# A first pair of token blocks taken from four of eight batches and computed beside the routing, with half-height token reads

## The chip, the cores and the metric

The kernel runs on one core of a Trainium2 chip. The metric is the device time of one execution in microseconds. Where a profile is quoted, PE is TensorE (PEld its weight loads), DVE is VectorE, ACT is ScalarE, POOL is GpSimd and SP is SyncE, which here only issues DMAs.

## The reference

Two parts run one after the other, all in float32. The first is a cross attention between 512 tokens and 32 states, per batch (8) and head (8, of width 64). The second is a mixture of 8 experts over the 544 rows (512 token reads and 32 state reads) of each batch, 4352 rows of width 512.

```python
scores = x @ state.T / 8;  a  = softmax(scores, states);  xread = a  @ state    # 512 rows
scores2 = state @ x.T / 8; a2 = softmax(scores2, tokens); sread = a2 @ x        # 32 rows
x = concat(xread, sread), heads side by side                                   # (8, 544, 512)

logits = x @ w_gate;  local_gate = sigmoid(x @ w_local)
for b in range(B):
    prev_e = -1
    for s in range(S):
        fresh_e = argmax(logits[b, s])
        e = fresh_e if s == 0 or local_gate[b, s] < 0.5 else prev_e
        prev_e = e
        out[b, s] = softmax(logits[b, s])[e] * (relu(x[b, s] @ w1[e]) @ w2[e])
```

A row whose gate is closed takes the expert of the row before it, so the choice is a scan along each batch. w1 is 512 x 1024 and w2 1024 x 512 per expert: 2 MB each.

## The kernel before

**Attention** (class `Attention`, from L180). The order of its steps on all engines is written out by hand in the string `STEPS`: each word is a step and a batch, with half of the heads (`u`) or a portion behind it. For a batch: `xt` and `xn` load x transposed and as it is (SP); `sc` computes the scores on PE; `mx`, `tr`, `mo` (DVE), `sb` (POOL), `ex` (ACT), `zh` (POOL), `zs`, `zi` (DVE), `ml` (POOL) and `tb` (DVE) make the softmax over the states; `et`, `tu`, `ec` and `sr` make the state reads. `lg` and `lt` give the logits of the token rows, `sl` and `sk` those of the state rows. `vv` computes the token reads (`token_reads`, L428): for each 128 tokens two matmuls, whose stationary operand is the shares `a` of four heads (4 x 32 = 128 rows) and whose moving operand `sd` holds those heads' states on the diagonal of a 128 x 256 matrix that is zero elsewhere. `xr` (ACT) copies the result, `wr` (SP) writes it to `rows`, a tensor in DRAM. The word `go` leaves the string; `reads()` goes on with it from the routing code, so that token reads of the last batches stand among the routing's instructions.

**Routing** (class `Routing`). When the logits of batches 0 to 6 are there, `choose` picks the largest for each row (L521 to L527), and again for batch 7. From there a serial chain runs, mostly on DVE: transposes, the scan along each batch (L557), one-hots of the expert, counts by matmul, the number of full 256-row pairs for each expert, the number of 32-row tiles for the rest, and a slot for each row (L642 to L661). One-hots of the slots, multiplied on PE (`slotted`, L710), turn slots into lists of rows: first for the first two blocks alone (`slots.two`), then for all blocks (`slots.tok`). `keep` (L538) issues dummy matmuls whose results nobody reads.

**Experts** (`experts`). Rows of one expert are worked off in pairs of blocks, 2 x 128 rows. POOL gathers a pair's rows (L821; `tick`, L835, ties a gather to a result on PE), SP loads the weights in quarters (L873). The first pair is multiplied in the plain way (`plain`, L1097), and its rows are gathered whole (L827) and turned on PE (`turned`, L856). Each later pair uses seven products of halves in place of eight (`strassen`, L1013, and `second_half`, L1053). Nine small tiles of 32 rows run between the first pairs. At least 10 pairs run unconditionally; each further one stands in a `tc.If` on the number of pairs (`last`). An indirect DMA on POOL scatters a block's 128 result rows to the output (L996). In the conditional pairs, the gather for the pair after next is issued before it is known whether that pair will run, and each scatter waits for the one before it to land, since both write `out`.

Of the kernel before, what the change touches and what calls it, by code (L numbers as in the profile page):

```python
# [40 lines left out]
NB = NP * 2  # L41
NBLK = NB + (NTILE + Q - 1) // Q
# [8 lines left out]
def kernel(  # L51
# [41 lines left out]
    route = Routing(ctx, tc)  # L93

    with ExitStack() as phase, ExitStack() as late:
        p = late.enter_context(tc.tile_pool(name="p", bufs=4, space=PSUM, side="right"))
        reads = late.enter_context(tc.tile_pool(name="reads", bufs=1, side="right"))
        lt = reads.tile([P, B, NC, SQ], F32, name="lt")
        with ExitStack() as early:
            make_identity(nc, ident)  # L100
            start = Attention(early, tc, p, reads, xn, xt, st, stt, wgl, wgs, lt, rows, none)
            route.constants(ident)
            start.clear()
            route.more_constants()
            start.run(route)
        bank = Banks(tc, 4)
        routing = route.route(bank, lt, slots, start.reads, rows)
        experts(phase, late, tc, bank, w1, w2, rows, slots, route, routing, out)
# [19 lines left out]
class Slots:  # L128


    def __init__(self, pool):

        self.tok = pool.tile([P, NBLK], I32, name="tok")
        self.two = pool.tile([P, 2], I32, name="two")

# [7 lines left out]
        self.experts = pool.tile([1, NP + NTILE - 1], I32, name="experts")  # L143
# [7 lines left out]
sc0 kp3 xt11 xt10 mx00 ga kp2 sd3 tr01 xt21 mx01 sd2 mo01 nb0 tr00 et01 sb01 xn0 mo00 wm14 sc1 et00 sb00 ex01  # L151
iv0 tu01 tr11 gl tu00 zh01 ex00 tr10 xt20 ec00 zh00 zs01 mo10 sd0 xn1 zs00 sb10 zi0 ec01 mx11 sd1 sr0 ml01 mo11
ex10 mx10 sc2 ml00 st0 xt30 tb01 rt0 sb11 tb00 sl0 xt31 tr20 lg0 nb1 ex11 zh10 sk0 tr21 vv03 et10 zh11 xt41 zs10
vv00 et11 lt0 mx21 xr03 xt51 zs11 tu11 zi1 xr00 tu10 iv1 ml11 mo21 vv02 xt50 ec10 mo20 ml10 sc3 ec11 tb11 xt40
xr02 mx20 sb21 sr1 tb10 xn2 tr30 sb20 ex21 lg1 mx30 st1 vv12 zh21 ex20 rt1 tr31 nb2 sl1 zh20 et20 vv10 zs21 sk1
lt1 ws1 zs20 et21 tu20 zi2 xt60 mo30 xr10 ml20 sc4 xr12 iv2 mx31 ec20 xn3 ml21 tu21 tb20 vv11 mx41 ec21 nb3 sb30
et30 tb21 sr2 tr40 et31 xt61 lg2 mo31 ex30 tu30 mo40 sb31 st2 sc5 lt2 wr00 xr11 mx40 ec30 zh30 tr41 wr03 tu31
ex31 nb4 zs30 sb40 vv23 et40 mx50 xt70 ec31 mo41 tu40 zh31 ex40 rt2 sr3 sb41 zs31 ws0 xr23 zi3 xn5 et41 iv3 sl2
ml31 mx51 vv22 ex41 sk2 iv4 st3 ml30 tb31 sc6 xr22 rt3 ec40 zh41 tb30 xt71 sl3 zh40 zs41 lg3 tr50 nb5 vv31 wr02
zs40 et50 zi4 vv01 xn4 lt3 xr31 ml40 mo50 sk3 tr51 xr01 vv13 ml41 tb40 et51 vv21 mo51 sb50 xr13 wr10 iv5 vv20  # L160
tb41 xr21 sb51 xn6 mx60 ex50 lg4 mx61 xr20 zh50 tu50 ex51 lt4 tu41 tr60 nb6 ec50 zh51 tu51 zs50 et60 mo60 vv32
wr20 ec51 zs51 sb60 zi5 tu60 ec41 wr23 tr61 sc7 xr32 ml50 wr11 ex60 mo61 sr4 et61 ml51 tb50 wr12 mx71 sr5 sb61
ws2 st4 tb51 ec60 ws3 vv30 tr70 zh60 ex61 xn7 mx70 st5 lg5 zh61 xr30 zs60 tu61 mo70 nb7 et70 vv40 zs61 sb70 zi6
ec61 tu70 lt5 wr22 iv6 xr40 ml61 rt5 sr6 rt4 ex70 tr71 wr40 ec70 ml60 mo71 sl5 et71 wr13 sl4 sk5 tb61 vv41 sb71
st6 wr31 tb60 tu71 zh70 ex71 sk4 iv7 wr32 lg6 rt6 xr41 zs70 zh71 sl6 ec71 lt6 wr21 vv42 zs71 zi7 wr01 sr7 sk6
xr42 ml71 ch0 wr42 vv33 st7 ml70 wr41 vv50 tb71 xr33 wr33 tb70 vv53 xr50 rt7 wr30 lg7 xr53 sl7 lt7 wr53 vv51 sk7
go wr50 vv43 xr51 wr51 go xr43 vv52 wr43 vv61 xr52 ws4 vv60 wr52 xr61 go ws5 xr60 vv62 wr60 go xr62 ws7 wr62
vv71 wr61 vv72 xr71 wr71 vv63 xr72 wr72 vv70 xr63 go wr63 go xr70 wr70 ws6 go vv73 xr73 wr73
# [3 lines left out]
class Attention:  # L172


    def __init__(self, ctx, tc, p, late, xn, xt, st, stt, wgl, wgs, lt, rows, none):
# [5 lines left out]
        self.xp = ctx.enter_context(tc.tile_pool(name="xp", bufs=3))  # L181
# [8 lines left out]
        self.sttc = [once.tile([P, n, KT, N], F32, name=f"sttc{i}") for i, n in enumerate((1, B - 1))]  # L190
# [3 lines left out]
        self.states_of = once.tile([P, B * G * DH], F32, name="states_of")  # L194
        nc.sync.dma_start(out=self.states_of, in_=st)
        nc.sync.dma_start(out=self.sttc[1], in_=stt[:, 1:])
        nc.sync.dma_start(out=wgs.rearrange("p w k e -> p (w k e)"), in_=wgl)
# [3 lines left out]
        self.sd = late.tile([P, B, G * GD], F32, name="sd", bufs=1)  # L201
# [10 lines left out]
    def clear(self):  # L212
# [5 lines left out]
        nc.gpsimd.memset(self.gl, 0.0)  # L218
        nc.gpsimd.memset(self.lt, 0.0)
        nc.gpsimd.memset(self.sd, 0.0)  # L220
# [9 lines left out]
    def reads(self):  # L230
# [7 lines left out]
                  sd=self.diagonal, ga=self.gates, gl=self.gates_kept, ch=self.choose, kp=self.keep, wm=self.warmed)  # L238
# [6 lines left out]
    def bank(self, parts=P, n=512):  # L245
        return self.p.tile([parts, n], F32, tag="p", name="p")
# [15 lines left out]
    def choose(self, i):  # L262
        self.route.choose(self.lt, 0, B - 1)

    def diagonal(self, k):
        r = slice(32 * k, 32 * k + 32)
        to = self.sd[r].rearrange("p b (g d) -> p b g d", g=G)
        self.nc.scalar.copy(to[:, :, :, DH * k:DH * k + DH],
                            self.states_of[r].rearrange("p (b g d) -> p b g d", b=B, g=G))

    def load_t(self, b, h):
        x = self.new(self.xp, f"x_t{h}", (b,), [P, KT // 2, S])
        self.nc.sync.dma_start(out=x.rearrange("p k s -> p (k s)"), in_=self.xt[b][:, h * D * 2:(h + 1) * D * 2])

    def load_n(self, b):
        x = self.new(self.xp, "x_n", (b,), [P, SC, G, KT, DH])
        self.nc.sync.dma_start(out=x.rearrange("p c u k d -> p (c u k d)"), in_=self.xn[b])

    def states(self, b):
        return self.sttc[b > 0][:, b - (b > 0)]  # L280
# [102 lines left out]
    def state_reads(self, b):  # L383
# [3 lines left out]
        for u in range(G):  # L387
            for c in range(SC):
                for k in range(KT):
                    self.nc.tensor.matmul(r[32 * k:32 * k + 32, u, :], lhsT=e[:, c, u, 32 * k:32 * k + 32],  # L390
                                          rhs=x_n[:, c, u, k, :], start=(c == 0), stop=(c == SC - 1))
# [36 lines left out]
    def token_reads(self, b, c):  # L428
        v = self.of["v", b, c] = self.bank()
        for u in range(G):  # L430
            d = slice(u * GD, u * GD + GD)
            self.nc.tensor.matmul(v[:, d], lhsT=self.get("a", b, u)[:, c * P:c * P + P], rhs=self.sd[:, b, d],  # L432
                                  start=True, stop=True)

    def reads_kept(self, b, c):
        xr = self.new(self.late, "xr", (b, c), [P, D], bufs=12)
        v = self.get("v", b, c)
        self.nc.scalar.copy(xr.rearrange("p (k u d) -> p u k d", k=KT, u=G),  # L438
                            v.rearrange("p (u k d) -> p u k d", u=G, k=KT))

    def reads_to_rows(self, b, c):
# [3 lines left out]
        t = b * T + c * P  # L445
        self.nc.sync.dma_start(out=self.rows[t:t + P].rearrange("t q x -> t (q x)"), in_=self.get("xr", b, c))
# [783 lines left out]
```

## Time and profile before

| | |
|---|---|
| median of 3 runs | 550.08 us (547.25 to 551.04) |
| the profiled execution | 546.65 us |
| its span, first to last instruction | 544.9 us |
| PE busy | 524.6 us (96%) |
| DVE busy | 382.5 us (70%) |
| POOL busy | 313.0 us (57%) |
| ACT busy | 174.0 us (32%) |
| moved by DMA | 155.48 MB, 285 GB/s over the span |
| mean granted PE clock | 0.987 |

The span is divided by what runs in it: attention to 68 us, routing to 95 us, expert pairs to 535 us, and the last scatters. An engine's share over the whole span says little, since the stages have different limits; the busy times by stretch are what to read. "Busy" for PE counts dummy matmuls too. Matmul ends are modelled, so the price of a matmul is better read from the distance of two starts, or from a long group's time divided by its count, than from a mean duration.

### The profile page before, as it was taken

To read this page: it belongs to the slowest core of one execution; us is meant where nothing else is said; L and a number is where in the kernel's file an instruction comes from. 1 tells how busy PE (TensorE), PEld (TensorE's weight loads), DVE (VectorE), ACT (ScalarE), POOL (GpSimd) and SP (SyncE) were. 2 spreads that over 40 slices of the span, in tenths; PEclk is the share of its full clock that TensorE was granted. 3 is DMA by queue.
4 is the path that set the end of the run, shared out by engine and by line. 5 is a ranking of instruction groups with operands and counts; after the bars stand their busy time and mean duration, and the time that the engine had idled before them with its cause. 6 is when DMAs were issued, how large, how long until landed. Compare 5 with 4: busy or idle time off the path is not lost. (4 is left out here: it accounts for less than half of the span.)

```text
span 544.9 us, 12958 instructions
## 1 busy us (share of the span) xinstructions
PE 524.6 (96%) x4916; PEld 459.3 (84%) x4916; DVE 382.5 (70%) x623; ACT 174.0 (32%) x359; POOL 313.0 (57%) x386
## 2 busy tenths in 40 slices
PE   8799898999999999999999999999999999999992
PEld 2567766989989898989898989899999998999992
DVE  6999876738575667575756658495776777777763
ACT  6788654111313232222222222223222221322230
POOL 7788602655574567565655556446565655445555
PEclk9999998999999999999999999999999999999997
DMA  8999766799989898898989898874748475565742
GB/s 320 410 350 350 294 237 214 275 397 390 377 284 387 299 376 322 327 369 299 375 294 369 293 366 299 320 251 142 259 142 302 134 276 178 216 218 205 248 151 99
DMA packets 49003, 155.48 MB, mean 285 GB/s; under 512 B 6865, under 2 KB 8017, under 8 KB 45602
## 3 DMA queue, kind: packets, MB, share of 16 engines
q1 hardware_dynamic: 41234, 135.78, 68.5%
q0 software_dynamic: 7552, 18.69, 9.6%
q8 instruction: 42, 0.69, 0.5%
q14 instruction: 31, 0.25, 0.1%
q10 hardware_dynamic: 144, 0.07, 0.1%
HBM read 136.68 MB, written 17.89 MB: 284 GB/s over the span
## 5 line engine op out<-in xcount | busy, mean ns | idle before, releaser
L821 POOL DMA_INDIRECT xg<-rows,row x132 | 157.4, 1192 | 29.5 <-issue 27.3
L930 DVE TENSOR_TENSOR a<-a,a 128x1024 f32<-128x1024 f32 x64 | 77.0, 1223 | 31.2 <-DMA a<-in_w_dram 29.8
L1013 PE MATMUL ps<-xt,a 128*128 128x128 f32 x720 | 88.6, 276 | 0.0
L1013 PE MATMUL sum<-xs,a 128*128 128x128 f32 x720 | 87.7, 275 | 0.0
L1013 PEld LDWEIGHTS ps<-xt,a 128*128 128x128 f32 x720 | 84.4, 192 | 2.1 <-issue 1.8
L1013 PEld LDWEIGHTS sum<-xs,a 128*128 128x128 f32 x720 | 84.0, 192 | 0.0
L930 DVE TENSOR_TENSOR c<-c,c 128x1024 f32<-128x1024 f32 x64 | 75.4, 1219 | 3.7 <-DMA c<-in_w_dram 3.2
L1053 PE MATMUL ps<-c,h 128*128 128x256 f32 x312 | 74.7, 382 | 0.0
L1053 PEld LDWEIGHTS ps<-c,h 128*128 128x128 f32 x312 | 58.0, 190 | 10.9 <-issue 3.7
L996 POOL DMA_INDIRECT out_dram<-y,tok x32 | 35.0, 1093 | 52.8 <-issue 16.8
L1053 PE MATMUL ps<-c,hs 128*128 128x256 f32 x256 | 60.5, 379 | 0.0
L1053 PEld LDWEIGHTS ps<-c,hs 128*128 128x128 f32 x256 | 48.6, 190 | 6.6
L1053 PE MATMUL sum<-c,h 128*128 128x256 f32 x200 | 47.2, 379 | 0.0
L930 DVE TENSOR_TENSOR h<-s,s 128x512 f32<-128x512 f32 x15 | 10.4, 693 | 51.5 <-ACT s L1036 48.2
L1053 PEld LDWEIGHTS sum<-c,h 128*128 128x128 f32 x200 | 38.0, 190 | 5.2
L849 DVE STREAM_TRANSPOSE xt<-xg 128x512 f32<-128x512 f32 x32 | 34.2, 1091 | 8.4 <-DMA xg<-rows,row 8.4
L964 ACT COPY sum<-ps 128x256 f32<-128x256 f32 (+1 forms) x31 | 14.3, 460 | 71.1 <-PE ps L1013 49.5
L835 POOL COPY tick<-s 1x1 f32<-1x1 f32 x45 | 15.9, 354 | 36.3 <-ACT s L1036 36.3
L835 POOL COPY tick<-r 1x1 f32<-1x1 f32 x41 | 17.2, 419 | 30.5 <-ACT r L1058 22.9
L432 PE MATMUL p<-sd,a 128*128 128x256 f32 x128 | 32.1, 390 | 0.2 <-ACT xr L438 0.2
L1058 ACT ACTIVATE r<-sum,prob 128x256 f32<-128x256 f32 x32 | 15.1, 473 | 52.0 <-PE sum L1053 49.5
L1053 PE MATMUL sum<-c,hs 128*128 128x256 f32 x128 | 30.2, 379 | 0.0
(230 smaller groups left out, 757.8 us busy)
## 6 DMA issues: line engine op xcount, KB each, us to landing
a<-in_w_dram SPq DMA_DIRECT2D x68, 512.0 KB
c<-in_w_dram SPq DMA_DIRECT2D x68, 512.0 KB
at<-in_w_dram SPq DMA_DIRECT2D x18, 1024.0 KB
ct<-in_w_dram SPq DMA_DIRECT2D x18, 1024.0 KB
x_t<-in_xt_dram SPq DMA_DIRECT2D x16, 512.0 KB
x_n<-in_xn_dram SPq DMA_DIRECT2D x8, 1024.0 KB
rows<-xr SPq DMA_DIRECT2D x32, 256.0 KB
xg<-rows,row POOLq DMA_INDIRECT x132, 5.7
```

The source lines that it names most:

```text
L432: self.nc.tensor.matmul(v[:, d], lhsT=self.get("a", b, u)[:, c * P:c * P + P], rhs=self.sd[:, b, d], start=True, stop=True)
L821: nc.gpsimd.indirect_dma_start(out=to.rearrange("p x k -> p (x k)"), out_offset=None, in_=rows.rearrange("n q x -> (n q) x"), in_offset=ba ...
L835: nc.gpsimd.tensor_copy(tick, value)
L849: nc.vector.transpose(to.rearrange("p k (i t) -> p k i t", i=Q), xgs_[u % 2][:, b].rearrange("p i x k -> p k i x"))
L930: nc.vector.tensor_tensor(out, a, b, op=op)
L964: nc.scalar.copy(y, x)
L996: nc.gpsimd.indirect_dma_start(out=out, out_offset=to, in_=y, in_offset=None, bounds_check=NT - 1, oob_is_err=False)
L1013: nc.tensor.matmul(to[:, m * P:m * P + P], lhsT=w[:, j, m * P:m * P + P], rhs=x[:, j, :], start=begin and m == 0 and j == 0, stop=(m == FK ...
L1053: nc.tensor.matmul(to, lhsT=x[:, m, :], rhs=w[:, m, :], start=begin and m == 0, stop=(m == FK // 2 - 1), skip_group_check=True)
L1058: nc.scalar.activation(to, t, Act.Copy, scale=p)
```

## The change

1. The commonest expert among the token rows of batches 0 to 3 is found as soon as these batches have logits (`EB` = 4). Its first 256 rows are gathered, its weights loaded into the buffers that held x, and both layers are computed in the plain way while attention and routing go on (class `Early`, new). The results wait in `ye`; they are scaled and scattered inside the first pair of the loop, when the probabilities are known.
2. The routing of all rows leaves these 256 rows out and counts one pair as done (the scan over pairs starts at 1.0). The loop has one pair less; its first pair is still computed in the plain way.
3. Token reads work on two heads at a time: 64 rows of `a` against a 64 x 128 block of `sd`, in the upper and lower half of the array, into two PSUM banks. `sd` is loaded by four DMAs into the two diagonal halves, in place of four ACT copies. Rows are written 256 at a time.
4. `STEPS` is a new string, and the early pair's steps stand in it, also behind the `go`s. The `keep(22)` and `keep(3)` of the routing are gone.
5. At the end: scatters in the conditional pairs are declared independent of each other, and a pair's last gather for a pair that may not run moves behind the `tc.If`. The tiles s and r of a pair share buffers.

```diff
-sc0 kp3 xt11 xt10 mx00 ga kp2 sd3 tr01 xt21 mx01 sd2 mo01 nb0 tr00 et01 sb01 xn0 mo00 wm14 sc1 et00 sb00 ex01
+lb lc sc0 kp3 la xt10 mx01 mx00 xt11 tr00 ga nb0 mo00 et00 xt20 tr01 sb00 gl tu00 mo01 et01 xn0 sb01 ex00 sc1
...
+wr31 fc ml41 kp4 tu50 ml40 mo50 ec50 wr21 fd tb41 sc6 fe sb50 ff tb40 xn4 fg ex50 mx60 lg4 fh zh50 vv41 lt4 fi
...
+fo xt71 rt4 sb51 tr60 sl4 sr5 fp et60 xn6 sk4 mo60 fq ex51 tu60 tr61 st5 mo61 et61 rt5 kp1 sc7 ec60 zh51 iv6
...
+ws7 tb71 pp011 wr50 sk7 cc lg7 cd ce pp012 lt7 wc1 go pp013 wc2 go rl01 vv60 wc3 pp100 xr601 xr600 pp101 wc0 go
+vv61 wr60 pp102 xr610 xr611 go pp103 wr61 pp000 rl10 pp001 pp002 vv71 go go qq1000 xr711 xr710 pp003 wr71 go
+qq1001 rl00 vv70 qq0000 xr701 xr700 qq0001 qq1010 wr70 go qq0010 qq0011 go qq0100 qq1011 qq1100 go qq1101 go
+qq1110 qq1111 qq0101 ye1 qq0110 qq0111 ye0
...
-        self.sd = late.tile([P, B, G * GD], F32, name="sd", bufs=1)
+        self.sd = late.tile([P, B, G, 2, DH], F32, name="sd", bufs=1)
...
+    def load_states(self):
+        st = self.inputs[1].rearrange("p (b u d) -> p b u d", b=B, u=G)
+        for k in range(KT):
+            r = slice(32 * k, 32 * k + 32)
+            self.nc.sync.dma_start(out=self.sd[r, :, :, k % 2, :], in_=st[r])
...
+    def token_reads(self, b, j):
+        v = self.of["v", b, j] = [self.bank().rearrange("p (c k u d) -> p c k u d", c=2, k=2, u=G) for h in range(2)]
+        for c in range(2):
+            t = slice((2 * j + c) * P, (2 * j + c) * P + P)
+            for u in range(G):
+                for h in range(2):
+                    r = slice(64 * h, 64 * h + 64)
+                    self.nc.tensor.matmul(v[h][:, c, :, u, :], lhsT=self.get("a", b, u)[r, t], rhs=self.sd[r, b, u],
+                                          start=True, stop=True)
...
+class Early:
...
+    def gather(self):
+        for k in range(2):
+            self.nc.gpsimd.indirect_dma_start(
+                out=self.first[k], out_offset=None, in_=self.rows[:EB * T].rearrange("n q x -> n (q x)"),
+                in_offset=bass.IndirectOffsetOnAxis(ap=self.slots.first[:, k:k + 1], axis=0))
...
+    def one(self, b, n, i):
+        if i == 0:
+            self.hps[b, n] = self.bank()
+        for j in range(KT):
+            self.nc.tensor.matmul(self.hps[b, n][:, i * P:i * P + P], lhsT=self.ring[0][2 * n + j // 2][:, j % 2, i * P:i * P + P],
+                                  rhs=self.x_t[:, j, b * P:b * P + P], start=(j == 0), stop=(j == KT - 1))
...
+    def two(self, b, n, o, s):
+        if (n, o, s) == (0, 0, 0):
+            self.yps[b] = self.bank()
+        for m in range(2 * s, 2 * s + 2):
+            self.nc.tensor.matmul(self.yps[b][:, o * D // 2:o * D // 2 + D // 2], lhsT=self.h[2 * b + n][:, m, :],
+                                  rhs=self.ring[1][2 * n + o][:, m, :], start=(n, o, m) == (0, 0, 0),
+                                  stop=(n == 1 and m == FK // 2 - 1), skip_group_check=True)
...
-        nc.vector.tensor_tensor_scan(end[:, 0], on[:, 0, 1:E + 1], pairs, 0.0, Alu.mult, Alu.add)
+        nc.vector.tensor_tensor_scan(end[:, 0], on[:, 0, 1:E + 1], pairs, 1.0, Alu.mult, Alu.add)
...
-        reads()
-        keep(22)
...
-        keep(3)
...
     next(routing)
+    load(0, 0)
+    gather_first()
+    next(routing)
+    reads()
+    turned_first(0)
+    next(routing)
+    reads()
     late.close()
...
+        if apart:
+            tc.declare_no_dep(put.ins, group="scatters", reason="a token has one slot, so scatters write other rows")
+            tc.add_to_no_dep_group("scatters", put.ins)
...
+                for b in range(2):
+                    nc.scalar.activation(early.ys[b], early.ys[b], Act.Copy, scale=slots.prob[:, b:b + 1])
+                    scatter(b, early.ys[b])
...
+        if not late:
+            calls = iter(range(NP))
+            gets[1] = lambda value: rest(value) if next(calls) < Q - 1 else None
```

In the new string, `fa` to `fr` are the early routing (transposes, scan, one-hots, counts, the commonest expert, ranks, place masks, list of rows, gather), `wa` and `wc` load its weights, `ta` and `tc` turn the gathered rows, each `pp` is four written matmuls of the first layer, each `qq` two of the second, `rl` and `ye` the copies behind them.

## The prediction

> **What bounds the kernel now.** First the page's slices, for where TensorE is short of work:
>
> ```profile
> span 544.9 us, 12958 instructions
> ...
> PE   8799898999999999999999999999999999999992
> ...
> PEclk9999998999999999999999999999999999999997
> DMA  8999766799989898898989898874748475565742
> ```
>
> From slice 8 (about 100 us) to the last one PE is full, so there the time is PE's work. The page's chain of waits holds 5% of the span and all of that in the tail, so it can't tell about the start. For that I took the busy times by stretch (columns: stretch, its length, busy us and count of PE, PEld, DVE, ACT, POOL, granted clock, DMA share, GB/s):
>
> ```profile
> 0.00:8.00 8.00, 6.15 (x26) 1.60 (x27) 4.22 (x18) 3.60 (x12) 6.73 (x13) 1.00 0.72 247
> 8.00:62.20 54.20, 49.27 (x1001) 33.89 (x1001) 51.28 (x123) 44.89 (x101) 43.34 (x54) 1.00 0.98 372
> 62.20:68.30 6.10, 5.11 (x103) 4.23 (x103) 5.09 (x13) 2.86 (x6) 2.26 (x2) 1.00 0.63 233
> 68.30:95.05 26.75, 23.93 (x174) 17.39 (x173) 19.12 (x64) 13.32 (x31) 2.96 (x3) 0.92 0.65 227
> 95.05:111.20 16.15, 16.15 (x136) 16.15 (x135) 11.93 (x22) 2.69 (x6) 10.40 (x11) 0.92 0.81 286
> ```
>
> Attention (8 to 68.3) is bound by DVE (56.4 busy of 60.3) with DMA close behind (0.98 up to 62.2). From 68.3, where the last batch's experts are chosen, to 95.05, where the first expert matmul starts, a serial routing chain runs; PE's 23.9 there are about 14 of token reads and 6.3 of dummy matmuls (L538). After that PE alone counts. Third, PE's timeline, for the unit prices:
>
> ```profile
> 95.08 5.08 PE L1097 MATMUL ps<-xt,a 128*128 128x128 f32 x32
> ...
> 100.47 10.88 PE L1097 MATMUL ps<-xt,a 128*128 128x128 f32 x96
> ```
> ```profile
> 485.80 1.95 PE L1013 MATMUL ps<-xt,a 128*128 128x128 f32 x16
> ...
> 508.66 1.89 PE L1053 MATMUL ps<-c,h 128*128 128x256 f32 x8
> 510.39 1.95 PE L1013 MATMUL ps<-xt,a 128*128 128x128 f32 x16
> ```
>
> A seven-product pair repeats after 510.39 - 485.80 = 24.6 us. A 128-column record takes 10.88/96 = 0.113 (0.159 in the first 32, under the lower clock), a 256-column one (510.39 - 508.66)/8 = 0.216. Each written fp32 matmul is two records. Last, two views for the edits: PE's groups up to 105 us, and the end of POOL.
>
> ```profile
> L432 PE MATMUL p<-sd,a 128*128 128x256 f32 x128 | 32.1, 390 | 0.2 <-ACT xr L438 0.2
> ...
> L307 PE MATMUL s<-x_t,sttc 64*32 64x512 f32 x128 | 9.8, 601 | 0.7 <-DMA x_t<-in_xt_dram 0.7
> ```
> ```profile
> 535.04 1.02 POOL L996 DMA_INDIRECT out_dram<-y,tok  x1 [0.30 <-issue]
> 536.03 0.81 POOL L835 COPY tick<-y 1x1 f32<-1x1 f32 x1
> 537.00 1.80 POOL L821 DMA_INDIRECT xg<-rows,row  x1 [0.16 <-issue]
> 540.07 1.02 POOL L996 DMA_INDIRECT out_dram<-y,tok  x1 [1.27 <-DMA out_dram<-y,tok]
> ```
>
> PE ends at 535.15; the last scatter goes out at 540.07, behind a gather that nobody will use and the landing of the scatter before it.
>
> **A pair less in the full stretch: -24.6.** The before trace holds 720/48 = 15 seven-product pairs and one plain one. Worked through the reference, the commonest expert of the first four batches has 512 token rows, so the early pair is full, its expert's remainder stays what it was, and the loop runs 15 pairs in place of 16. The first pair of the loop stays plain, so one seven-product pair goes.
>
> **Attention gets longer: +5.5 on DVE, +1 at the start.** Added before the last batch's choice, priced by the same operation in the old routing: a scan over 512 columns 1.2 (the 8x544 one took 1.27), one-hots 0.25 (half of 0.49), two place masks 1.25 (four took 2.49), some 14 small operations at 0.15 to 0.2, 2.4; choosing in three portions instead of two 0.4. Sum 5.5, on the bound engine. The lower end is 1.6, if it falls in the 3.9 that DVE idles between 8 and 68.3; I take 5.5, since those idles are waits of 0.2 to 1 us that new operations don't fit. ScalarE loses the four diagonal copies (4.2) and gains about 7 of copies and activations by the end of attention; it has 9 free. POOL gets two gathers at 1.1 and three small operations, about 3, in 11 free. At the start SP now waits for a halved clear of the state tile (3.5/2, ending near 4.0) and issues four loads (about 0.45 each) ahead of batch 1's x, which it issued at 3.47 before and near 6.5 now. Batch 1's scores ran at 12.15 on that load, with DVE idle 1.0 for them. Bounds 0 to +3; I take +1, as less is queued beside it. The logits of batch 7, 67.1 before, then run at 73.6.
>
> DMA has to agree: issued up to batch 7's x are 8.4 MB of transposed x, 6.3 of the other, 4.2 of finished rows and 1.3 of states, 20.2 MB. With 2.8 moved by 10 us and 0.39 MB/us after that (before: 281 GB/s in the first 10 us, 351 to 415 in the next four stretches of 10), that is 55 us. Some 40 DVE operations of 0.45 follow it, so 73 to 74. At 0.36 it is 58, and everything 3 later.
>
> **Token reads.** 128 records of 256 columns (27.7 at 0.216) become 256 of 128 columns on half of the rows. If two halves run side by side, 13.8 to 14.5; if not, 28.9. L307's 64x32 tiles are the nearest row: 16 records of 512 columns took 1.09, where 16 x 0.432 = 6.9 would be serial, so halves and columns do overlap; I take 1.0 for each group of 16, 16 in all. Of these 12 lie in attention, beside DVE, and gain nothing; 4 lie in routing. In L307, 16 weight loads took 0.18, or 11 ns each, so loads of separate tiles overlap too.
> The Trainium skill, "TensorE: Matmul & The Clock Gate", section "LDWEIGHTS (loading the stationary operand)", speaks against this edit: a load costs its columns at 1.2 per ns, however few rows it has. By that 256 loads of 128 columns are about 27 us (an estimate from that page), the edit gains nothing, and the routing stretch is 2.8 longer; L307's 11 ns, where the rule gives 27, is why I don't take it.
>
> **The routing stretch becomes PE-bound: 26.75 to about 38.** PE keeps its order, and behind batch 7's logits it now has: 10 early steps of 8 records (0.91) = 9.1; 16 of 4 records of 256 columns (0.864) = 13.8; four token reads 4.0; the logits 1.0; the chain's own matmuls 9.3 (transposes 0.57 and 0.42, counts 0.6, ends and experts 0.46, 40 for two blocks 2.0, 40 for all blocks 3.9, quarter rows 0.54, turns and bank claims about 0.9). Sum 37.2, plus 1 for hand-overs. The new work is cut into portions of 0.9 to 6 us between chain steps, each about the DVE work there (3.3 of count arithmetic beside 4.6, 6 of slot arithmetic beside 6.2), so DVE hides behind PE. The 25 removed dummies are worth 0: the matmul behind them waited for DVE at 85. First loop matmul at 73.6 + 38.2 = 111.8, against 95.05: **+16.7**. Bounds: 104 (DVE additions hidden, gaps none) and 122 (start +3, DMA +3, reads serial +3, hand-overs +1).
>
> **First plain layer: -1.2.** It took 16.15; at full clock with both blocks there, 128 x 0.113 and 0.6 of turns is 15. The early pair's scaling (two ScalarE copies near 0.6) and two scatters (2.1) go into POOL's 5.7 free there; uncovered they cost 2.
>
> **Tail: -3.9.** Without the unused gather and the wait between scatters, the last one goes out near 536.2 instead of 540.07.
>
> **Sum.** +16.7 - 24.6 - 1.2 - 3.9 = -13.0. The profiled execution was 546.65 (span 544.9 and 1.75 around it), so 533.6 for its like; the median of the runs shown is 3.4 above it, so 537 for the median.
>
> **Rivals.**
> *POOL stalls (slower).* The early gather needs the rows of four batches in DRAM, and behind it on POOL stand the subtractions and shares of batches 5 to 7, for which DVE and ScalarE wait. The rows' last write is about 17 MB into the queue, 46 us; the gather is due near 54. If it waits, each us of it moves everything: from 13 on the change loses. Before, the wait of the token read (L719) for the rows was 18.7, though with nothing behind it. With 20 lost, 557. Against it: 8 us of slack.
> *PSUM instead of PE.* A token read now takes two of four banks, and an early product holds one; if each of 16 reads waits for a 0.58 copy, +9, and 546.
> *Reads don't overlap.* +3 in routing and up to 3 in attention: 541 to 543.
> *Early routing is hidden.* Loop from 104: 529.
>
> **How the numbers follow.** Forecast, 532 to 542 with the serial reads in it: 0.60. Hidden: 0.10. PSUM or late DMA, 544.6 to 551: 0.16. POOL stall or the like, above 555.6 mostly: 0.14. Range 529 to 551 leaves out about 0.2. A measurement here can tell 1%, 5.5 us: faster 0.70, same 0.16, slower 0.14.
>
> **What would show it.** After: 14 seven-product pairs spaced 24.6; batch 7's logits near 74; the first loop matmul near 112 with PE full and clock 1.00 before it; L468 groups of 16 near 1.0 us; two final scatters about 1 us apart. Wrong, if the logits come after 80, if PE idles over 5 us between them and the loop, or if POOL waits for rows before the early gather.

## The result and the profile after

The changed kernel took 551.34 us (median of 20 runs, 549.15 to 556.11), the kernel before 549.48 us (20 runs) beside it: a ratio of 1.0049, 95% interval 1.0026 to 1.0073. Forecast were 537 us and a gain of 2.4%. So a loss of half a per cent came of it, within what the text called no change. The profiled execution took 551.26 us, its span is 549.5, against 546.65 and 544.9 before.

The page of the changed kernel, its span and the slices of PE, its granted clock and the DMA engines (each digit is a fortieth of the span, in tenths):

```profile
span 549.5 us, 13280 instructions
...
PE   6998899999989999999999999999999999999995
...
PEclk9898899999999999999999999999999999999998
DMA  9999899469969798998979797978646483846662
```

PE is full from slice 6 (69 us) on but for slice 12 (151 to 165 us), which is looked at below. So the loss is in what comes ahead of the loop and in how much shorter the loop became. The same kernel by stretches up to the first loop matmul, which starts at 122.59 (95.05 before); the columns are the stretch, its length, the busy time of each engine, PE's granted clock, the DMA share and GB/s:

```profile
0.00:8.00 8.00, 6.17 (x26) 1.61 (x27) 2.88 (x20) 3.60 (x12) 5.01 (x13) 1.00 0.73 215
8.00:74.40 66.40, 57.27 (x1147) 36.97 (x1145) 56.09 (x138) 43.08 (x103) 42.69 (x55) 0.92 0.95 327
74.40:83.95 9.55, 9.28 (x157) 8.51 (x157) 6.21 (x20) 5.14 (x12) 6.30 (x7) 1.00 0.98 343
83.95:97.00 13.05, 13.05 (x145) 12.02 (x146) 8.19 (x34) 4.20 (x10) 0.00 (x0) 1.00 0.87 306
97.00:122.59 25.59, 23.60 (x194) 20.28 (x190) 16.80 (x53) 10.12 (x23) 3.97 (x4) 1.00 0.54 177
sum 122.59, PE 109.38 PEld 79.39 DVE 90.17 ACT 66.14 POOL 57.97; mean PE 21.88 PEld 15.88 DVE 18.03 ACT 13.23 POOL 11.59
```

The early pair's first product starts at 74.3 and batch 7's logits at 83.95 (67.08 before). Read the third row against the others: from 74.4 on PE is busy in 45.9 of 48.2 us, and DVE, which set the pace of attention before, is not. And read the sum: up to the loop PE is busy for 109.4 us, against 84.5 of 95.05 before. Of the 27.5 us by which the loop starts later, 24.9 are PE's busy time and 2.6 its idle time. That is a sum and not yet a cause. Over attention alone, from 8 us to batch 7's logits, neither engine is full; the rows are before, after, and e4, a kernel of the experiments that is the same up to these logits:

```profile
8.00:67.08 59.08, 53.16 (x1077) 37.05 (x1078) 55.99 (x132) 47.75 (x107) 45.60 (x56) 1.00 0.95 360
8.00:83.95 75.95, 66.56 (x1303) 45.48 (x1301) 62.30 (x157) 48.22 (x114) 48.99 (x61) 0.93 0.96 329
8.00:83.66 75.66, 63.44 (x1300) 44.23 (x1298) 62.28 (x157) 48.37 (x114) 48.93 (x61) 1.00 0.96 331
```

What PE does there, groups of matmuls between 8 us and the loop (records, then busy time and mean ns, then idle time before them), first before, then after:

```profile
L432 PE MATMUL p<-sd,a 128*128 128x256 f32 x128 | 32.1, 390 | 0.2 <-ACT xr L438 0.2
...
L307 PE MATMUL s<-x_t,sttc 64*32 64x512 f32 x112 | 7.6, 601 | 0.1
```

```profile
L468 PE MATMUL p<-sd,a 64*128 64x128 f32 x256 | 18.2, 283 | 0.1
L643 PE MATMUL p<-xt,x 128*128 128x128 f32 x128 | 16.4, 280 | 0.3 <-DMA x<-in_w_dram 0.3
L653 PE MATMUL p<-x,h 128*128 128x256 f32 x64 | 15.3, 387 | 1.2 <-ACT h L647 1.2
L339 PE MATMUL s<-x,sttc 64*32 64x512 f32 x114 | 12.9, 780 | 0.6 <-DMA x<-in_xt_dram 0.6
```

The token reads give back 13.9 us (32.1 to 18.2), the early pair's two layers cost 31.7, and the scores, which the change doesn't touch, cost 5.3 more: a batch's 16 records take 1.09 us when both halves of x have landed, but batch 4's came as two runs of eight, 1.5 us apart, and took 2.56, and batch 7's took 1.96 while the granted clock was 0.61 (65 to 69 us).

From there to the end the two kernels compare like this:

| | before | after | difference | forecast |
|---|---|---|---|---|
| first loop matmul | 95.05 | 122.59 | +27.5 | +16.7 |
| of it: batch 7's logits | 67.08 | 83.95 | +16.9 | +6.5 |
| of it: logits to loop | 27.97 | 38.64 | +10.7 | +10.2 |
| first plain layer | 16.14 | 14.84 | -1.3 | -1.2 |
| rest of the loop | 423.96 | 405.29 | -18.7 | -24.6 |
| last matmul to the end | 9.75 | 6.8 | -2.9 | -3.9 |
| span | 544.9 | 549.5 | +4.6 | -13.0 |

The rest of the loop falls short by 5.9, and here is where, in the order of time on PE in the changed kernel (start, duration, group, idle time before it):

```profile
157.04 0.25 PE L1006 MATMUL ps<-pd,turn 128*128 128x9 bf16 x4
157.22 1.29 PE L1159 MATMUL ps<-ct,htt 128*32 128x128 f32 x39
158.79 0.43 PE L1159 MATMUL ps<-ct,htt 128*32 128x128 f32 x5 [0.28 <-issue]
159.52 0.43 PE L1159 MATMUL ps<-ct,htt 128*32 128x128 f32 x4 [0.30 <-issue]
160.26 0.44 PE L1159 MATMUL ps<-ct,htt 128*32 128x128 f32 x6 [0.31 <-issue]
```

The 64 matmuls of a tile's second layer took 1.95 us at each of the nine tiles in the trace of before. Here the first takes 5.65, and four others 2.1 to 3.0; the nine sum to 23.1 us against 17.6. "Issue" says that PE waited for nothing that the profile shows.

The tail on POOL after:

```profile
538.84 0.97 POOL L1094 DMA_INDIRECT xg<-rows,row  x1 [0.38 <-issue]
540.13 1.02 POOL L1239 DMA_INDIRECT out_dram<-y,tok  x1 [0.32 <-DVE y L1319]
543.60 1.73 POOL L1239 DMA_INDIRECT out_dram<-y,tok  x1 [2.44 <-DVE y L1326]
```

The unused gather and the wait for the first scatter's landing are gone. The second scatter now waits for DVE's last result and goes out 3.5 us after the first, not 1.

### The profile page after: what moved, and what is told of

It reads as the page before. It is cut to its first block, busy times and chain, and to the rows that moved or that the text cites. A ratio compares the mean times of both kernels' runs of the same rounds, so it can differ in the third digit from the quotient of the medians.

```text
span 549.5 us, 13280 instructions
## 1 busy us (share of the span) xinstructions
PE 527.2 (96%) x5104; PEld 458.2 (83%) x5104; DVE 369.2 (67%) x633; ACT 169.5 (31%) x357; POOL 311.3 (57%) x373
## 4 chain that ended last, share of the span: by engine, by line
PE 87%; DMA 5%; DVE 4%; issue 1%; SPq 1%; POOL 1%; ACT 0%; POOLq 0%; ACTq 0%; DVEq 0%
PE ps L1299 21%; PE ps L1259 19%; PE sum L1259 14%; PE sum L1299 12%; PE ps L1159 4%; PE ps L1147 3%; PE ps L1343 3%; PE p L643 3%; PE p L653 2%; DMA x<-in_xn_dram 2%; DMA x<-in_xt_dram 2%; PE ps L942 2%; PE s L339 1%; DMA x<-in_w_dram 1%; PE p L468 1%
## 5 line engine op out<-in xcount | busy, mean ns | idle before, releaser
L1259 PE MATMUL sum<-xs,x 128*128 128x128 f32 x608 | 74.1, 275 | 0.0
L1259 PE MATMUL ps<-xt,x 128*128 128x128 f32 x592 | 73.3, 277 | 0.0
L1259 PEld LDWEIGHTS ps<-xt,x 128*128 128x128 f32 x592 | 69.6, 192 | 1.9 <-issue 1.4
L1259 PEld LDWEIGHTS sum<-xs,x 128*128 128x128 f32 x608 | 70.9, 192 | 0.0
L1173 DVE TENSOR_TENSOR x<-x,x 128x1024 f32<-128x1024 f32 x49 | 59.1, 1220 | 10.9 <-DMA x<-in_w_dram 9.9
L1239 POOL DMA_INDIRECT out_dram<-y,tok x30 | 36.6, 1219 | 17.6 <-DVE y L1326 9.6
L1103 POOL COPY tick<-r 1x1 f32<-1x1 f32 x38 | 17.8, 469 | 38.2 <-ACT r L1304 35.6
L1299 PE MATMUL ps<-c,h 128*128 128x256 f32 x160 | 38.3, 382 | 0.0
L1299 PEld LDWEIGHTS ps<-c,h 128*128 128x128 f32 x160 | 29.8, 190 | 5.8 <-issue 2.1
L1299 PE MATMUL ps<-c,hs 128*128 128x256 f32 x144 | 34.0, 379 | 0.0
L1299 PE MATMUL ps<-x,h 128*128 128x256 f32 x136 | 32.6, 382 | 0.0
L1299 PEld LDWEIGHTS ps<-x,h 128*128 128x128 f32 x136 | 25.3, 190 | 4.8 <-issue 1.6
```

The costliest lines, as they stand in the source:

```text
L1103: nc.gpsimd.tensor_copy(tick, value)
L1173: nc.vector.tensor_tensor(out, a, b, op=op)
L1239: put = nc.gpsimd.indirect_dma_start(out=out, out_offset=to, in_=y, in_offset=None, bounds_check=NT - 1, oob_is_err=False)
L1259: nc.tensor.matmul(to[:, m * P:m * P + P], lhsT=w[:, j, m * P:m * P + P], rhs=x[:, j, :], start=begin and m == 0 and j == 0, stop=(m == FK ...
L1299: nc.tensor.matmul(to, lhsT=x[:, m, :], rhs=w[:, m, :], start=begin and m == 0, stop=(m == FK // 2 - 1), skip_group_check=True)
```

## The experiments

All times of milestones are from one profiled execution each. Five of the kernels here are the same up to the loop (the changed kernel, and those altered in the loop only). In the four of them that are used for it, batch 7's logits run from 81.58 to 83.95 and the loop starts from 120.23 to 122.59: differences below 2.4 us in these two say nothing.

**Is it the loads?** Three kernels. e1 loads the states in one DMA of long runs, with four ScalarE copies into the diagonal in their place:

```diff
-        for k in range(KT):
-            self.nc.sync.dma_start(out=self.sd[r, :, :, k % 2, :], in_=st[r])
+        self.nc.sync.dma_start(out=self.states_of, in_=self.inputs[1])
+    def diagonal(self, k):
+        self.nc.scalar.copy(self.sd[r, :, :, k % 2, :],
+                            self.states_of[r].rearrange("p (b u d) -> p b u d", b=B, u=G))
```

> The changed kernel with its states loaded as before, in one DMA of 4 KB runs, and put on the diagonal halves by four ACT copies. Theory A (late x: the end of attention is set by when the x of the late batches lands): the four loads of 64-float runs held the DMA engines at a share of 1.24 for 240 GB/s between 8 and 12 us, where the kernel before moved 416; 0.7 MB less there and 0.3 MB less between 4 and 8 us are worth about 2.5 us, so the logits of batch 7 come at 81 to 82 instead of 83.95, and the total falls by 2 to 3 us. Theory B (attention is set by VectorE's added work and by the order of steps): the logits stay within 1 us of 83.95.

Logits at 82.16, loop at 120.80, 551.14 us against 550.26 (ratio 1.0019, 0.9987 to 1.0051): within the spread. e2 leaves out 2 MB of the loads:

```diff
+            if h == 0 or b not in (3, 4, 5, 6):
                 self.nc.sync.dma_start(out=x, in_=self.xn[b][:, h * D * 2:(h + 1) * D * 2])
```

> The changed kernel without the second half of the x loads for the state reads of batches 3 to 6 (the matmuls run on the values that are in the buffers): 2 MB less, 1.5 MB of it ahead of batch 7's transposed x. Theory A: at the 0.34 MB/us that the changed kernel moved between 10 and 64 us, that x lands 4.4 us earlier and the logits of batch 7 come at 79 to 80. Theory B: 83 to 84, since no VectorE instruction and no step of the order is changed.

Logits at 82.84, loop at 121.48. The DMA share from 60 to 72 us fell from 0.80 to 0.49 and nothing beyond the spread followed from it, so the bytes don't set attention's end. e3 moves steps of batches 6 and 7 up in the order:

```diff
 xt60
+xt61 xt70
...
 wr30
+xt71
...
+sc7
 fo
...
 tr61
+mx70
 mo61
+mx71
```

> The changed kernel with the transposed x of batches 6 and 7 issued before the rows of batches 2 and 3 on SP, and with batch 7's scores and maxima moved up in the order of steps. Theory A with SP's order as the cause: batch 7's scores run near 58 to 60 instead of 65.86, its logits 3 to 6 us earlier (78 to 81), the total falls by as much. Theory A with the sum of bytes as the cause: what is moved ahead pushes the rest back, so the scores come earlier, the logits at 83 to 85. Theory B: as the latter.

Logits at 88.33, loop at 126.95, ratio 1.0136 (1.0037 to 1.0235; four runs). The one load moved up (batch 7's scores came at 64.58) pushed the others back: PE waited 4.4 us for batch 4's natural x. e8 moved the load of the states behind batch 0's natural x:

```diff
-lb lc sc0 kp3 la
+lb sc0 kp3 la
...
 xn0
+lc
```

> The changed kernel with the load of the states (four DMAs of short runs) moved from the first place in SyncE's queue to behind batch 0's natural x, so that it no longer stands ahead of batch 1's transposed x. If that load is what makes batch 1's scores 1.9 us late (14.04 us against 12.16), sc1 comes at 12.0 to 12.6 and batch 3's logits at 43 rather than 44.9. What follows for batch 7: theory A' (loads) gives 82 us for its logits, theory C 83 to 84, since the early chain starts from batch 3's logits but batches 4 to 7 then wait for the chain all the same: the two differ by no more than the spread of the milestones here, so this run only prices the start, at 0 to 2 us.

Batch 1's scores came at 11.27, 2.8 us earlier, and the clock in 12 to 24 us was 1.00 in place of 0.86; the logits stayed at 83.88, the loop at 122.52. The better start is lost again long before batch 7: batch 3's logits came at 45.01, against 43.66 in the changed kernel.

**Is it PE's own work?** e4 leaves 12 of the 16 early second-layer steps out:

```diff
+        if n or s:
+            return
         for m in range(2 * s, 2 * s + 2):
```

> The changed kernel without 12 of the 16 steps of the early pair's second layer (48 records of 256 columns, 10.4 us of PE). If PE bounds the stretch from batch 7's logits to the first loop matmul, 38.6 us falls to 28 or 29. If the serial chain on VectorE or the hand-overs bound it, it stays above 35.

Logits at 83.66, loop at 117.17, 33.5 us behind them in place of 38.6: of 10.4 us taken away 5.1 were gained. PE was then busy in 15.3 of the last 20.2 us, at a granted clock of 0.80 in place of 1.00, so part of the loss may be the clock. With that said, PE's work is not all that holds the stretch: some of it is the routing's chain of steps.

**Is it the early choice, or the token reads?** Four kernels make a table of the two. e7 drops the choice and takes fixed rows and expert 0; e13 drops the reads of batches 0 to 3; e12 drops both; e11 drops the choice and e2's 2 MB.

```diff
-        return dict(fa=self.sequence, fb=self.holds, fc=self.filled, fd=self.back, fe=self.experts_kept,
+        return dict(fa=self.fixed, **{f"f{c}": lambda: None for c in "bcdefghijklmnopr"}, fq=self.gather,
...
```

```diff
+        for name in ("vv", "xr", "wr"):
+            do[name] = lambda b, *at, step=do[name]: step(b, *at) if b >= EB else None
```

> The changed kernel without its early choice: the steps from the sequence to the chosen slots are left out, the first pair takes rows 0 to 255 and expert 0, and the later routing counts all tokens (so the first pair's rows of the output are not the reference's). All loads, all attention steps, the token reads, the gather and the first pair's products stay. Theory C (the early routing chain, 6.3 us of DVE work and its hand-overs from engine to engine, stands in order between the steps of batches 4 to 7 and holds them up): batch 7's logits come at 77 us or earlier (83.95 in the changed kernel), the loop's first matmul at 113 to 117. Theory A' (the later loads and the order of steps alone set the end of attention): logits at 82 to 84, loop at 120 or later. DVE's busy time from 44 to 84 us falls by about 6 us under either.

> Both suspects taken away at once: no early choice (as e7) and the second half of natural x of batches 3 to 6 left out (as e2, 2 MB less). Each alone moved batch 7's logits by 1.1 to 1.4 us only (82.56 and 82.84 against 83.95). Theory G (two chains of about the same length, the DMA queue's and the early routing's, so that either alone holds the end): logits at 77 or earlier. Rival H (neither is the limit; the token reads of batches 0 to 3, which now stand within the attention stage with their ScalarE copies and their writes in SyncE's queue, hold the loads behind them): logits at 80 to 82.

> No early choice (as e7), and the token reads of batches 0 to 3 with their copies left out; their rows are written as zeros after the attention stage, and the early gather takes its rows from natural x. So the attention stage holds nothing of the change but the loads in halves, the order of steps and the first pair's products. Theory H: logits of batch 7 at 68 to 72 (67.08 before). Rival G, or an order of steps that is slow in itself: 76 or later.

> The early choice stays, the token reads of batches 0 to 3 are left out (as e12, with zeros written afterwards and the early gather from natural x). Theory H alone: logits of batch 7 at 74 to 76, that is those of e12 and the 5 to 6 us of the early choice's VectorE work. If the early choice holds batches 4 to 7 up by its waits once the loads are on time: 79 or later.

| batch 7's logits | with the choice | without |
|---|---|---|
| with the reads | 83.95 | 82.56 (and 82.12 without 2 MB of loads) |
| without the reads of batches 0 to 3 | 81.62 | 78.72 |

Theories C, G and H fall, each by its own number: the choice alone is within the spread, and even without choice and reads the logits come 11.6 us later than before. The choice costs 2.9 us once the reads are out, the reads 3.8 once the choice is out, and both together 5.2. (e12's and e13's loop and time are not read: the zeros written behind attention delay the routing.)

**Is it a milestone at all?** e15 moves the six early product steps that stand ahead of batch 7's logits behind them; e14 leaves the fillers out. Both have an edit in the loop as well, read further below.

In `STEPS`, first e15, then e14 (what stands between these words is left as it is):

```diff
-pp110 pp111 pp112 pp113 rl11 pp010 pp011
...
 lg7
+pp110 pp111 pp112 pp113 rl11 pp010 pp011
```

```diff
-kp3 kp5 kp2 kp4 kp2 kp1 kp1
```

> Two edits. The six early product steps that stand ahead of batch 7's logits on PE (6.3 us) are moved behind them. Theory P: the logits come 5 to 6 us earlier, near 78, and the loop starts where it did, 121 to 124, since PE has the same work before it. Rival O (batch 7's logits set the loop, 38.6 us behind them): the loop starts at 115 to 118. In the loop, the last tile's scatter stands apart (as e10): on a chip where the tenth seven-product pair is late (27.8 to 31.4 us in e7 to e9), theory F gives 24.6 here and 27 or more for e14.

> Two edits at places far apart. In the attention stage the filler matmuls (18 of 0.39 us, 5.3 us of PE in the changed kernel's trace, which compute nothing) are left out. Theory P (PE's own work sets the start of the loop): the first loop matmul comes 3 to 5 us earlier, 118 to 120, with batch 7's logits at 80 to 82. Rival O (the order of steps and its waits set it): PE idles instead, the loop stays at 121 to 123; if the fillers hold up the clock, it comes later than 123. In the loop, the early pair's two scatters stand behind the third pair (as e9). On a chip where the tiles' second layer is slow, theory D gives 2.0 to 2.6 us for the first tile's here and about 5 for e15's; rival D' gives 5 for both.

e15's logits of batch 7 came in two halves, the last at 81.38, 2.6 us earlier, and its loop started 2.6 us later, at 125.17. Its row for 72 to 84 us, and e14's for 12 to 24 (columns as above):

```profile
72.00:84.00 12.00, 8.92 (x160) 7.36 (x159) 9.04 (x30) 5.34 (x12) 7.47 (x9) 0.86 1.00 367
```

```profile
8.00:12.00 4.00, 0.24 (x8) 0.15 (x8) 3.71 (x6) 0.78 (x2) 1.43 (x3) 0.88 1.23 239
12.00:24.00 12.00, 10.38 (x232) 5.67 (x232) 7.36 (x16) 6.30 (x16) 7.32 (x9) 0.64 0.95 379
```

In e15 PE idles 3.1 us where the product steps had stood, and has them still to do afterwards: the loop starts 43.8 us behind the logits instead of 38.6. Had the logits alone set the loop, it would have started 2.6 us earlier. e14's 5.3 us of fillers less made the logits (86.42) and the loop (125.06) 2.5 us later, just outside the spread, so theory P, that PE's work alone sets the loop, falls too: without the fillers PE's clock was 0.64 from 12 to 24 us and 0.72 from 48 to 72, against 0.74 to 0.86 and 0.86 to 1.00 in five kernels that have them (the changed one, e9, e10, e15 and e18). The Trainium skill, "TensorE: Matmul & The Clock Gate", section "What's actually happening", says that the array falls to half its clock after an idle window of some 3.4 us; the row of 0.24 us busy in 4 and the one behind it fit that.

The milestone is one where the order is kept. In eleven runs whose order of steps behind batch 7's logits is that of the changed kernel (it, e1 to e3, e7 to e11, e14 and e18) the loop starts 38.63 to 38.65 us behind them, while the logits lie anywhere from 81.58 to 88.33. So what attention loses, the loop's start loses whole; and the stretch behind changes when PE's work is moved into it (e15) or out of it (e4).

**The loop: the tiles' slow steps.** e9 moves the early pair's scaling and scatters from behind the loop's first pair to behind its third:

```diff
             if u == 0:
                 next(probabilities)
+            if u == 2:
                 for b in range(2):
```

> The changed kernel with the early pair's scaling and its two scatters moved from behind the loop's first pair to behind its third. In the changed kernel and in e1 to e3 the first tile's second layer takes 4.8 to 6.2 us in place of 1.95. Theory D (POOL and the DMA rings do seven indirect transfers in a row there, because the second scatter waits for ScalarE and holds up the gathers behind it, and PE's instructions come late beside them): the first tile's second layer falls to 2.0 to 2.6 us, the time by about 3.5 us to 546, unless the third tile's takes the stall over. Rival D' (the first run through the tile's code is late whatever stands beside it): it stays at 5 us or more, and the time at 549 to 551.

All nine tile steps took 1.95 us, but so they did in e7 and e8, which have the scatters in the old place. These ran on another chip than e1 to e4. Over all runs the kernels with the slow steps (23.1 us for nine, or 19.8 to 24.3) are those of three sessions in which the kernel before took 549.5 to 550.3 us, and those without them (17.6) of three sessions in which it took 547.1 to 547.4. e16 and e19 profiled the kernel before beside others:

> The kernel before itself, profiled on the same chip as the other two. If the slow second layer of the tiles is the chip's, the first tiles' take 2.1 to 5 us here too (1.95 in the first trace of before) on a chip where e14 or e15 show it. If it comes with the change, all nine take 1.95 to 1.96 here while e15's first takes 4.7 or more. On a chip that shows it in neither, this run says nothing.

> The kernel before, profiled beside them. On the first kind of chip: nine tile steps of 1.95 if the stall comes with the change, several above 2.1 if it is the chip's. On the second kind: as e16, nine of 1.95.

Both fell on chips of the second kind and showed 1.95 nine times. So theory D was not tried where it could show, and whether the kernel before has slow steps on a chip of the first kind stays open.

**The loop: one late pair.** On chips of the second kind the loop lost about as much in another place. The tenth seven-product pair took 31.31 us in e9, 29.27 in e8 and 27.81 in e7, in place of 24.6. (On the first kind it was late in e1 and e4, beside slow tile steps, and not in the others.) e14's PE there:

```profile
416.15 1.95 PE L1258 MATMUL ps<-xt,a 128*128 128x128 f32 x16
422.09 2.26 PE L1258 MATMUL ps<-xs,x 128*128 128x128 f32 x9 [3.99 <-DVE xs L1172]
```

DVE waited 8.9 us for the gathered rows at that time. e14's POOL, which issues the gathers:

```profile
398.56 1.01 POOL L1238 DMA_INDIRECT out_dram<-y,tok  x1 [0.30 <-issue]
404.36 1.19 POOL L1168 DMA_INDIRECT out_dram<-yt,row  x1 [4.80 <-DVE hs L1272]
405.55 0.40 POOL L1102 COPY tick<-y 1x1 f32<-1x1 f32 x1
406.10 1.82 POOL L1093 DMA_INDIRECT xg<-rows,row  x1 [0.16 <-issue]
```

The last tile's scatter (L1168) stands idle for 4.8 us between the pair's scatters and the gathers. The change put this tile into the first of the last pairs, whose scatters are declared independent of one another; the tile's is not, and waits for their landing. The engine named there, DVE, is only the last event seen; in the changed kernel's own trace the same wait is put down to the DMA of `out_dram` (2.61 us there, with the tenth pair on time). e10 declares that scatter independent too:

```diff
+            if self.i == NTILE - 1:
+                tc.declare_no_dep(put.ins, group="scatters", reason="a token has one slot, so scatters write other rows")
+                tc.add_to_no_dep_group("scatters", put.ins)
```

> The changed kernel with one more scatter let go ahead: the last tile's scatter stands apart from the others too. In e1, e4, e7, e8 and e9 the tenth seven-product pair takes 27.8 to 31.4 us in place of 24.6, because its gathered rows come late; POOL reaches those gathers only after the last tile's scatter, which waited for the landing of the pair's scatters before it. Theory F (that wait is what makes the gathers late): the tenth pair takes 24.6 to 25.5, the time falls to 543 to 546, the ratio to the kernel before lies under 1. Rival F' (the gathers are late because of the weights queued ahead of them in the DMA rings): the tenth pair still takes 27 us or more, and the time stays at 548 to 551.

This ran on a chip of the first kind: 553.27 us, ratio 1.0068 (1.0039 to 1.0096), tile steps of 23.5 us, and a tenth pair of 24.6, as e11 to e13 have it there without the edit. So it told nothing. e15 carries the same edit, and ran on one chip of the second kind with e14. The same place on POOL in e15:

```profile
398.67 1.00 POOL L1241 DMA_INDIRECT out_dram<-y,tok  x1 [0.30 <-issue]
399.97 0.98 POOL L1168 DMA_INDIRECT out_dram<-yt,row  x1 [0.30 <-issue]
400.93 0.18 POOL L1102 COPY tick<-y 1x1 f32<-1x1 f32 x1
401.27 1.01 POOL L1093 DMA_INDIRECT xg<-rows,row  x1 [0.16 <-issue]
```

The gathers start 4.8 us earlier, and the tenth pair takes 24.6 against 31.37 in e14. Three runs on one chip set the changed kernel, both loop edits together, and the kernel before side by side:

> The changed kernel unaltered, on the chip of e18 and e19. On the first kind of chip: tile steps of 4.7 to 6 us at the first tile, time 551 to 553. On the second: nine tile steps of 1.95, a tenth pair of 28 to 31.4, time 548.5 to 550.5, a ratio to before of 1.003 to 1.006.

> The changed kernel with two edits in the loop: the last tile's scatter stands apart (as e10 and e15), and the early pair's two scatters stand behind the third pair (as e9). On the second kind of chip theory F gives a tenth pair of 24.6 and 543 to 545 us, a ratio to before of 0.990 to 0.996. On the first kind theory D gives a first tile step of 2.0 to 2.6 us and 546 to 549 us; rival D' 5 us and 551 to 553.

The changed kernel 550.44 us, ratio 1.0035 (1.0014 to 1.0055). With the scatter freed 544.17 us, ratio 0.9927 (0.9900 to 0.9954), before 547.27 and 547.31 (e19). So the two edits together are worth 6.3 us on such a chip, and turn the change from a small loss into a small gain. That it is the declaration is read from the tenth pair: it takes 24.6 in e15, which has only this edit in the loop, and about 31.3 in e9 and e14, which have only the other.

**The tail alone.** e5 is the kernel before with the change's tail and nothing else:

```diff
+                tc.declare_no_dep(put.ins, group="scatters", reason="a token has one slot, so scatters write other rows")
+                tc.add_to_no_dep_group("scatters", put.ins)
...
+            gets[1] = lambda value: rest(value) if next(calls) < Q - 1 else None
+            with tc.If(pairs > u + 1):
+                rest()
```

> The kernel before with nothing of the change but its tail: the scatters of the conditional pairs stand apart from one another, and the last speculative gather is moved behind the If. If the tail's share of the change is what the two traces show (9.75 us from the last matmul to the end before, 6.8 after), this comes out 3 us under the kernel before, 546 to 547.5 us, with the last scatter issued within 4 us of the last matmul and nothing else moved. If the tail's gain came from the rest of the change (other buffers, one pair less), the time stays at that of before, within 1 us.

544.12 us against 547.36: ratio 0.9936 (0.9908 to 0.9964). The last matmul ended at 537.07 and the span at 543.5, so the tail is 6.5 us in place of 9.75.

## Why the prediction was wrong

**The step that failed is "Attention gets longer: +5.5 on DVE, +1 at the start", hence logits at 73.6.** They came at 83.95, and these 10.4 us are nearly all of the 10.8 by which the loop started later than forecast. (The span missed its forecast by 17.6 us; 5.9 more are in the loop and 1.0 in the tail.) The terms were sound: DVE's busy time from 8 us to the logits grew by 6.3 (55.99 to 62.30), and batch 1's scores came 1.9 us later. What it took for granted was that DVE would stay the bound and idle no more than before. DVE idled 13.7 us there, against 3.1. By stretch: 8 to 24 us 4.3 (1.6 before), 24 to 48 2.1 (0.5), 48 to 72 3.9 (1.1 to the logits), and 3.4 in the last 12 us, where PE is full of early products. Its waits there were 6.0 us for scores from PE, 5.7 for ScalarE and 1.6 for POOL. The step never made up PE's account for attention either: PE had been busy in 53.2 of 59.1 us there, and the change puts the choice's matmuls, the turns and six product steps into the same queue ahead of batch 7's logits.

But PE doesn't pace attention by its work. It is busy in 66.6 of 76.0 us, and in e4, at a granted clock of 1.00 in place of 0.93, in 63.4 of 75.7, with the logits 0.3 us earlier. Nor are the early products the cause of the late logits. The logits of batches 3 to 7 started at 41.59, 46.70, 54.05, 60.07 and 67.08 before, and at 43.66, 55.46, 71.43, 79.98 and 83.95 after: 2.1, 8.8, 17.4, 19.9 and 16.9 later. So all of the delay is there by batch 5's, at 71.43, ahead of the first product at 74.3. In e12, without choice and reads, batch 5's still come at 66.16.

What the runs put in its place: an attention stage in which no engine is full and the steps of several engines wait for one another, most of all between batch 3's and batch 5's logits, with a stretch of 38.6 us behind it in which PE is nearly full (36.7 us busy). What stays open is the cause of the 10 us: no single thing left out (loads, choice, reads, start) moved the logits beyond the spread, and two together moved them by 5.2 us. The remaining 11.6 us go with what e12 keeps of the change, the new order of steps above all, which no run took back; that the order is the cause was not shown. The step's check by DMA took 0.39 MB/us for granted; the trace has 330 GB/s from 24 to 48 us and 316 from 48 to 72. But 2 MB less (e2) moved the logits by 1.1 us only, so the lower rate by itself does not set attention's end.

The Trainium skill, "Perfetto Trace Analysis", section "Identifying the Most-Contended Engine", warns that PE's matmul busy share is a poor measure of how near a kernel is to its limit. e4 is in line with that, with 5.1 us gained of 10.4 busy us removed: the account says that PE is full behind the logits, not that each us in it is worth one.

**A pair less, -24.6:** right in the trace of e18, where the loop from its first matmul to its last is 414.2 us against 439.8 in e19, 25.6 less (forecast 24.6 + 1.2). In the changed kernel about 6 are lost again, by slow tile steps on some chips and by the late pair on others. The text looked for POOL's waits ahead of the loop, at the early gather; it didn't ask what the tile that moved into the last pairs would wait for.

**The routing stretch:** 38.6 against 38.2, with PE full in the first 13 us and 92% busy in the rest. **Plain layer:** -1.3 against -1.2. **Tail:** -2.9 against -3.9, as the second scatter waits 2.4 us for DVE, which the text had overlooked.

**Token reads:** priced at 1.0 us for a group of 16 records. A group lasts 1.16, two in a row 2.1, and all 256 records 18.2 us where 16 were forecast. The rule weighed against this, from "TensorE: Matmul & The Clock Gate", section "LDWEIGHTS (loading the stationary operand)", gives 27 us for them; the measurement decides against it here.

**The rivals.** POOL's early gather waited 0.21 us for rows: that rival fell. So did the one of PSUM (PE waited 0.5 us in all for the copies of reads) and that of reads that don't overlap. "Routing hidden" fell too. The condition under "wrong, if the logits come after 80" was met, by a cause for which the list had no rival: an attention stage full of waits between engines.

**Against each other:** without the late pair the whole change is worth 0.7% (e18), and its tail alone 0.6% (e5). What moving a pair of products beside the routing gained, 25.6 us less of loop, was paid back by a start that is 24.8 us later in e18 (121.17 against 96.34). The best kernels of the study are these two, with nothing to choose between them.

## What to carry to other kernels

Before work is moved beside a stage, make up each engine's account over that whole stage: busy time there now, plus what comes, minus what goes, against its length. Here PE was busy in 53.2 of 59.1 us and DVE in 56.0; work was priced on DVE alone, and the stage became 16.9 us longer for 6.3 us more of DVE's work, with both engines idle more than before. Price the waits that a new order makes as well, and look at which batch or step first comes late before blaming work that stands behind it. When some of a set of scatters are freed from one another, look for the one that stands among them and was left out: it waits for all of them, and everything queued behind it waits too.

## What the runs showed of the hardware

- The same program lost its time in different places on different chips: in three sessions nine tile steps of 64 short matmuls took up to 24.3 us in place of 17.6, with idle time that no semaphore explains, and in three others never. The kernel before was some 2.5 us slower in the former sessions too (549.5 to 550.3 us against 547.1 to 547.4).
- A wait of PE cost more than its length here. After 3.99 us of it in e14, the pair was 6.8 us late; in e9 the granted clock fell to 0.50 in the four us after such a gap and 0.68 in the next four.
- Matmuls on 64-row tiles for two heads run side by side with loads of 128 columns: 16 records in 1.16 us, where 16 of full height and twice the columns took 4.0 (32.1 us for 128).
